# A fixed order, slot by slot, for the instructions of a block (convolution, two matrix products, SiLU)

## The chip, the cores and the metric

One core of one Trainium2 chip. The metric is the device time of one execution in microseconds (us). Engines: PE (TensorE) multiplies matrices into PSUM, which has eight banks of 128 x 512 float32; DVE (VectorE) and ACT (ScalarE) work elementwise and can read PSUM; POOL (GpSimd) and the DMA queues move and prepare data.

## The reference

The input `x` has 8 sequences of 4096 tokens with 192 channels. A causal convolution over 7 tokens has one set of softmax weights for each of 8 heads (24 channels each). Then, token by token:

```python
attn = lightweight_conv(x, softmax(weight))   # (32768, 192)
h = attn @ w_in                               # 192 -> 2048
g = h * (1 / (1 + exp(-h)))                   # SiLU
out = g @ w_out                               # 2048 -> 192
```

The weights `w_in` and `w_out` arrive as float64 and are rounded to float32 on the chip. All arithmetic is float32.

## The kernel before

The 32768 tokens are cut into 32 blocks of 1024. A block is two halves of 512 tokens, which stand side by side in the Strassen-like form in which both matrix products are computed: instead of 12 plain products for one row of chunks there are 11, of sums of inputs and sums of weights, and the results are sums of products again.

*Convolution* (`turn_in`, `conv`, `spread`). The input of the next block is loaded as 32 x 32 squares (`load`, 12 DMAs), turned by three DVE transposes, and its halo copied by a DMA (`xt<-xt`). `conv` runs 7 taps for each of three channel groups `k`, on DVE, each tap adding to the one before. `spread` copies a finished group by four DMAs into the tile `dup`. `win` makes four DVE differences of `dup` in the tile `win`. Before the change `conv` and `turn_in` are generators, stepped by the callers.

*First product* (`up`, line 343). For each of 8 chunks `m` there are 11 products named P1 to P7 and E11 to E22, each with 64 rows of the array; two of them, one in the upper and one in the lower half of the array, run at the same time as a pair. `ORDER` (line 75) lists 44 pairs. The products of one `m` go into three banks, "1", "b" and "d". Bank "1" grows from P1 by P6, P7, P4 and E21, and is copied to a buffer `u` after P1 (ACT), P6 (DVE) and P7 (ACT) (`snap`, lines 377 and 379); the next product of that bank has to wait for the copy. `total` (line 384) adds such a copy and bank "b" or "d" on DVE (line 386) and applies SiLU on ACT (line 387); the chunk in bank "1" itself goes through SiLU directly (line 396). The buffers `u` are 8.

*Second product* (`sum_g`, `down`, `merge`). For each of four pairs of chunks `j`, `sum_g` makes four DVE sums of g (1024 elements wide, line 427), and `down` multiplies 22 times into five banks `accs`, two matmuls at the same time in the left and right half of the array. `merge` combines the five banks by 7 ACT copies and 6 DVE sums into `cmb`; `store` turns it by three DVE transposes and stores it by 12 DMAs.

*What sets the order.* A scheduler places each instruction on its engine's queue by its priority and by when its inputs are expected; program order is only a preference. `fill` (line 530) hands out steps of `store`, `turn_in`, `conv` and `sum_g` after every second slot of ORDER; the rest of `conv`, `spread`, the next `load` and `win` stand between the four `down`s. Banks and buffers are given out in the order in which they are first written. Block 0 is special: its first product is plain (`up_plain`), mixed with the rounding of the weights (`rounded`), and its POOL sums of weights come later.

Of the kernel before, what the change touches and what calls it, by code (L numbers as in the profile page):

```python
# [17 lines left out]
def kernel(  # L18
# [238 lines left out]
    def turn_in(b):  # L257
        nat = nats[b]
        xt = xts[b] = xpool.tile([P, NK, pad + TB], F32, tag="xt", name="xt")
        if b * TT % S == 0:  # L260
            nc.gpsimd.memset(xt[0:R, :, 0:pad], 0.0)
        else:
            nc.gpsimd.tensor_copy(xt[0:R, :, 0:pad], tails.pop(b))
        for k in range(NK):
            nc.vector.transpose(
                xt[:, k, pad : pad + TB], nat[:, k, :, :].rearrange("p k c -> p (k c)")
            )
            yield
        nc.sync.dma_start(out=xt[R:P, :, 0:pad], in_=xt[0:R, :, TB : TB + pad])
        if (b + 1) * TT % S:  # L270
            tails[b + 1] = xpool.tile([R, NK, pad], F32, tag="tail", name="tail", bufs=2)
            nc.sync.dma_start(out=tails[b + 1], in_=xt[R:P, :, TB : TB + pad])

    def conv(b, k):

        src = xts[b][:, k, :]
        dst = nats[b][:, k, :, :].rearrange("p k c -> p (k c)")
        for i in range(K):
            tap = taps[:, k, i : i + 1]
            if i == 0:  # L280
                nc.vector.tensor_scalar(dst, src[:, 0:TB], scalar1=tap, scalar2=None, op0=ALU.mult)  # L281
            else:
                nc.vector.scalar_tensor_tensor(  # L283
                    out=dst, in0=src[:, i : i + TB], scalar=tap, in1=dst, op0=ALU.mult, op1=ALU.add
                )
            yield
# [14 lines left out]
    def win(b):  # L301

        d = dups[b]
        t = wins[b] = xpool.tile([P, 4, TB], F32, tag="win", name="win")
        for i, u, v in (
            (0, d[:, 1, 0, :], d[:, 0, 0, :]),
            (1, d[:, 1, 1, :], t[:, 0, :]),
            (2, d[:, 1, 1, :], d[:, 1, 0, :]),
            (3, d[:, 0, 1, :], t[:, 1, :]),
        ):  # L310
            nc.vector.tensor_tensor(t[:, i, :], u, v, op=ALU.subtract)
# [31 lines left out]
    def up(b, fill):  # L343


        d, t = dups[b], wins[b]
        bk, us, seen = {}, {}, set()

        def product(m, name):
            e, r, s = m % 2, wr[m // 2], ws[m // 2]  # L350

            other, bn, w, v = {
                "P1": (0, "1", r[:, 0, 0, :], d[:, 0, 0, :]),
                "P6": (0, "1", r[:, 0, 1, :], t[:, 1, :]),
                "P7": (0, "1", r[:, 1, 0, :], t[:, 2, :]),
                "P4": (0, "1", r[:, 1, 1, :], t[:, 3, :]),
                "E21": (0, "1", r[:, 1, 2, :], d[:, 0, 2, :]),
                "P2": (1, "b", s[:, 0, 1, :], d[:, 0, 1, :]),
                "E11": (1, "b", s[:, 0, 2, :], d[:, 0, 2, :]),
                "P5": (1, "d", s[:, 1, 0, :], t[:, 0, :]),  # L360
                "E22": (1, "d", s[:, 1, 2, :], d[:, 1, 2, :]),
                "P3": (1, "d", s[:, 0, 0, :], d[:, 1, 1, :]),
                "E12": (1, "d", s[:, 1, 1, :], d[:, 1, 2, :]),
            }[name]
            half = e ^ other
            first = (m, bn) not in bk
            if first:
                bk[m, bn] = bank()
# [5 lines left out]
        def snap(m, i):
            us[m, i] = upool.tile([P, TB], F32, tag="u", name="u")
            if i == 2:
                nc.vector.tensor_copy(us[m, i], bk[m, "1"])  # L377
            else:
                nc.scalar.copy(us[m, i], bk[m, "1"])  # L379

        def g_of(m, a, n):
            return g_tile(b, m // 2, a)[:, n, m % 2, :]

        def total(m, a, n, i, bn):
            g = g_of(m, a, n)
            nc.vector.tensor_tensor(g, us[m, i], bk[m, bn], op=ALU.add)  # L386
            nc.scalar.activation(g, g, AF.Silu)  # L387

        after = (
            (("P1",), lambda m: snap(m, 1)),  # L390
            (("P6",), lambda m: snap(m, 2)),
            (("P7",), lambda m: snap(m, 3)),
            (("E22", "P7"), lambda m: total(m, 1, 1, 3, "d")),
            (("P3", "E12"), lambda m: total(m, 0, 1, 2, "d")),
            (("E11", "P1"), lambda m: total(m, 0, 0, 1, "b")),
            (("E21", "P4"), lambda m: nc.scalar.activation(g_of(m, 1, 0), bk[m, "1"], AF.Silu)),  # L396
        )
        for i, slot in enumerate(ORDER.split(", ")):
            new = []
            for one in slot.split():  # L400
                name, m = one.split(".")
                product(int(m), name)
                new.append((int(m), name))
            seen.update(new)
            for needs, what in after:
                for m, name in new:
                    if name in needs and all((m, n) in seen for n in needs):
                        what(m)
            fill(i)

    sums = {}

    def sum_g(b, j):

        t = [tpool.tile([P, 2, 2 * TB], F32, tag="t", name="t") for _ in range(2)]
        sums[b, j] = t
# [4 lines left out]
        for out, u, v in (
            (t[0][:, 0, :], of(0, 1), of(0, 0)),
            (t[0][:, 1, :], of(1, 1), t[0][:, 0, :]),
            (t[1][:, 1, :], of(1, 0), t[0][:, 1, :]),
            (t[1][:, 0, :], of(1, 1), of(0, 1)),
        ):
            nc.vector.tensor_tensor(out, u, v, op=ALU.subtract)  # L427
            yield

    def down(b, j, accs):  # L430
        g = [gs.pop((b, j, a)) for a in range(2)]
        t = [s.rearrange("p i (e t) -> p i e t", e=2) for s in sums.pop((b, j))]
# [7 lines left out]

        for e in range(2):
            for a in range(2):
                for n in range(2):
                    mm(0, n, w[:, a, e, 2 * R : D], g[a][:, n, e, :], e == 0 and a == 0)
        for i, one, two in (
            (1, (w[:, 0, :, 0:R], g[0][:, 0]), (x_[:, 1], t[0][:, 1])),
            (2, (w[:, 1, :, 0:R], g[1][:, 0]), (w[:, 1, :, R : 2 * R], t[1][:, 1])),
            (3, (x_[:, 2], g[1][:, 1]), (x_[:, 0], t[0][:, 0])),
        ):
            for e in range(2):  # L450
                for half, (lhs, rhs) in enumerate((one, two)):
                    mm(i, half, lhs[:, e, :], rhs[:, e, :], e == 0)
        for e in range(2):
            mm(4, e, w[:, 0, e, R : 2 * R], t[1][:, 0, e, :], True)
# [133 lines left out]
```

## Time and profile before

| | |
|---|---|
| median of 3 runs | 3277.9 us (3275.98 to 3287.45) |
| profiled execution | 3288.16 us, span 3286.4 us |
| PE busy | 2882.4 us, 88% |
| DVE busy | 2049.5 us, 62% |
| ACT busy | 1013.4 us, 31% |
| POOL busy | 57.4 us, 2% |
| mean granted clock of TensorE | 0.929 of full speed |

The profile shows one execution. Its span goes from the first to the last instruction. Matmuls are pipelined and their ends are modelled, so a busy PE need not be at full speed. PEld is the load of weights into the array, which overlaps the matmuls. An idle time is put down to the instruction whose end released it. L369 are the matmuls of `up`, L436 those of `down`, L331 those of block 0's `up_plain`.

### The profile page before, as it was taken

What the parts mean: (1) busy time and instruction counts of PE and PEld (TensorE: products, weight loads), DVE (VectorE), ACT (ScalarE), POOL (GpSimd) and SP (SyncE); (2) the same over time, 40 slices, a digit from 0 to 9 for tenths busy, and PEclk for the clock granted to TensorE, in tenths of its full rate; (3) what the DMA queues carried; (4) which work ended last, traced back from release to release, by engine and by line L of the source; (5) the groups of instructions that cost most, each with busy time, mean ns of one, the idle gap of its engine ahead of it and who ended that gap; (6) DMA issues with size and microseconds to landing.
All of it is one profiled execution on the core that took longest, in us unless ns stands there. A gap on an engine that the chain in (4) does not pass through costs nothing.

```text
span 3286.4 us, 29826 instructions
## 1 busy us (share of the span) xinstructions
PE 2882.4 (88%) x11280; PEld 1169.8 (36%) x11280; DVE 2049.5 (62%) x2758; ACT 1013.4 (31%) x1763; POOL 57.4 (2%) x105
## 2 busy tenths in 40 slices
PE   3998889888898988989888999889998898988998
PEld 2333333333333333333333333333333333333333
DVE  8756666656657566666566665665656657566644
ACT  2233322323322333223232223332233322333222
POOL 5100000000000000000000000000000000000000
PEclk9999998998999999999999999998999999999989
DMA  6211112211022110221111221102212022110110
GB/s 135 39 33 36 23 26 39 39 29 33 16 39 39 33 36 10 39 39 33 36 28 21 39 39 30 37 11 39 39 29 38 11 39 39 33 36 17 32 29 10
DMA packets 451296, 110.79 MB, mean 34 GB/s; under 512 B 423952, under 2 KB 424848, under 8 KB 451152
## 3 DMA queue, kind: packets, MB, share of 16 engines
q1 hardware_dynamic: 447872, 101.00, 16.7%
q0 software_dynamic: 1664, 5.51, 0.6%
q10 hardware_dynamic: 1616, 2.39, 0.3%
q8 instruction: 88, 1.44, 0.2%
q14 instruction: 56, 0.46, 0.0%
HBM read 31.49 MB, written 25.17 MB: 17 GB/s over the span
## 4 chain that ended last, share of the span: by engine, by line
PE 60%; DVE 31%; issue 5%; ACT 3%; DMA 1%; SPq 0%; DVEq 0%; ACTq 0%
PE ps L436 31%; PE ps L369 29%; DVE nat L283 11%; DVE t L427 5%; DVE g L386 4%; DVE u L377 4%; DVE cmb L463 2%; DVE u L463 2%; ACT g L387 1%; DVE nat L281 1%; DVE osb L485 1%; PE ps L331 1%; ACT u L379 1%; DMA nat<-in_x_dram 1%; ACT cmb L465 0%
## 5 line engine op out<-in xcount | busy, mean ns | idle before, releaser
L369 PE MATMUL ps<-dup,ws 64*128 64x512 f32 x2480 | 980.6, 625 | 0.0
L369 PE MATMUL ps<-win,wr 64*128 64x512 f32 x1488 | 761.4, 723 | 230.8 <-DVE u L377 206.8
L436 PE MATMUL ps<-g,wo 128*64 128x512 f32 x3072 | 901.4, 593 | 0.0
L386 DVE TENSOR_TENSOR g<-u,ps 128x512 f32<-128x512 f32 x744 | 495.5, 683 | 640.9 <-PE ps L369 547.9
L387 ACT ACTIVATE g<-g 128x512 f32<-128x512 f32 x744 | 465.9, 630 | 513.5 <-DVE g L386 504.8
L369 PE MATMUL ps<-dup,wr 64*128 64x512 f32 x992 | 566.8, 710 | 22.0 <-ACT u L379 20.5
L369 PEld LDWEIGHTS ps<-dup,ws 64*128 64x128 f32 x2480 | 406.3, 202 | 307.7 <-issue 285.4
L427 DVE TENSOR_TENSOR t<-g,t 128x1024 f32<-128x1024 f32 x256 | 313.4, 1224 | 292.0 <-PE ps L436 288.7
L436 PEld LDWEIGHTS ps<-g,wo 128*64 128x64 f32 x3072 | 284.5, 137 | 590.7 <-issue 567.2
L436 PE MATMUL ps<-t,wx 128*64 128x512 f32 x1024 | 481.2, 592 | 0.0
L369 PEld LDWEIGHTS ps<-win,wr 64*128 64x128 f32 x1488 | 284.1, 225 | 539.2 <-DVE u L377 281.0
L379 ACT COPY u<-ps 128x512 f32<-128x512 f32 x496 | 278.6, 583 | 508.2 <-DVE g L386 451.8
L283 DVE SCALAR_TENSOR_TENSOR nat<-xt,taps,nat 128x512 f32<-128x512 f32 x576 | 415.9, 745 | 6.4
L436 PE MATMUL ps<-t,wo 128*64 128x512 f32 x1024 | 372.1, 592 | 0.0
L369 PE MATMUL ps<-win,ws 64*128 64x512 f32 x496 | 292.3, 690 | 89.5 <-DVE g L386 89.5
L427 DVE TENSOR_TENSOR t<-g 128x1024 f32<-128x1024 f32 x256 | 304.9, 1222 | 43.1 <-ACT g L387 43.1
L465 ACT COPY cmb<-ps 128x512 f32<-128x512 f32 x32 | 18.7, 585 | 971.9 <-PE ps L436 971.9
L369 PEld LDWEIGHTS ps<-dup,wr 64*128 64x128 f32 x992 | 188.0, 217 | 203.9 <-issue 93.2
L436 PE MATMUL ps<-g,wx 128*64 128x512 f32 x512 | 240.6, 592 | 0.0
L396 ACT ACTIVATE g<-ps 128x512 f32<-128x512 f32 x248 | 142.4, 593 | 106.4 <-PE ps L369 102.9
L377 DVE COPY u<-ps 128x512 f32<-128x512 f32 x248 | 166.4, 681 | 0.0
L369 PEld LDWEIGHTS ps<-win,ws 64*128 64x128 f32 x496 | 88.9, 200 | 169.7 <-DVE g L386 115.1
(60 smaller groups left out, 1043.5 us busy)
## 6 DMA issues: line engine op xcount, KB each, us to landing
dup<-nat SPq DMA_DIRECT2D x384, 128.0 KB, 2.3
nat<-in_x_dram SPq DMA_DIRECT2D x384, 64.0 KB, 2.5
out_dram<-osb SPq DMA_DIRECT2D x384, 64.0 KB, 1.9
raw<-in_moe_w_out_dram POOLq DMA_DIRECT2D x8, 384.0 KB, 4.2
raw<-in_moe_w_in_dram POOLq DMA_DIRECT2D x12, 192.0 KB, 4.2
ws<-wr ACTq DMA_DIRECT2D x8, 192.0 KB, 4.3
raw<-in_moe_w_in_dram ACTq DMA_DIRECT2D x4, 192.0 KB, 8.0
xt<-xt SPq DMA_DIRECT2D x32, 4.5 KB, 1.9
```

The source lines that it names most:

```text
L281: nc.vector.tensor_scalar(dst, src[:, 0:TB], scalar1=tap, scalar2=None, op0=ALU.mult)
L283: nc.vector.scalar_tensor_tensor(out=dst, in0=src[:, i : i + TB], scalar=tap, in1=dst, op0=ALU.mult, op1=ALU.add)
L331: nc.tensor.matmul(hs[a, n, e], rows(wr[j], e)[:, a, k, :], rows(d, e)[:, n, k, :], start=k == 0, stop=k == NK - 1,)
L369: nc.tensor.matmul(bk[m, bn], rows(w, half), rows(v, half), start=first, stop=True, skip_group_check=True,)
L377: nc.vector.tensor_copy(us[m, i], bk[m, "1"])
L379: nc.scalar.copy(us[m, i], bk[m, "1"])
L386: nc.vector.tensor_tensor(g, us[m, i], bk[m, bn], op=ALU.add)
L387: nc.scalar.activation(g, g, AF.Silu)
L396: (("E21", "P4"), lambda m: nc.scalar.activation(g_of(m, 1, 0), bk[m, "1"], AF.Silu)),
L427: nc.vector.tensor_tensor(out, u, v, op=ALU.subtract)
L436: nc.tensor.matmul(accs[i][R * half : R * half + R, :], lhs, rhs, start=first and j == 0, stop=j == NJ - 1, skip_group_check=True,)
L463: nc.vector.tensor_tensor(out, u, v, op=ALU.add)
```

## The change

The order of a block is written out in one text, PLAN, of 88 slots: 44 for `up`, 44 for `down`. A slot names two products of `up`, or stands for two matmuls of `down`, and then the DVE and ACT instructions that follow them: `s` copies a bank, `C` adds, `g` applies SiLU, `t` is a sum of g, `i` and `v` are transposes and taps of the next block, `w` its window, `M`, `z`, `y`, `c` the merge, `o` an output transpose with its stores. A minus sign means the block before. `pin` ties each of these instructions behind the one traced before it on its engine, so that the queue has the order of the text. The products are in a new order, the buffers `u` are 13, the banks of `down` are taken when first used, and the last steps of a merge stand in the first slots of the next block's `up`. In block 0 the roundings are placed one ahead of each `up_plain`.

```diff
-    upool = ctx.enter_context(tc.tile_pool(name="up", bufs=8))
+    upool = ctx.enter_context(tc.tile_pool(name="up", bufs=13))
...
+    PLAN = (
+        "P1.0 P1.1 -z7.0 -M3.0 | P1.2 P5.0 s1.1 -M4.0 | P5.1 E22.0 s1.0 -M5.0 s1.2 | "
+        "E22.1 P6.1 -M6.0 | P6.0 P1.3 s2.1 | P6.2 P5.2 -o.0 s1.3 s2.0 | P5.3 P7.1 s2.2 | "
+        "P7.0 E22.2 -o.1 s3.1 | P7.2 P6.3 i.0 s3.0 C22.1 | E22.3 E21.1 s3.2 s2.3 | "
+        "P4.0 P4.1 g22.1 C22.0 | E12.1 P7.3 C22.2 g22.0 | E21.0 E12.0 i.1 C21.1 s3.3 i.2 | "
+        "E21.2 E12.2 C21.0 C22.3 | P3.1 P3.0 g22.2 | P4.2 P4.3 g22.3 C12.0 | "
+        "E12.3 P2.0 C12.1 g12.0 | P2.1 E11.0 v.00 C21.2 v.01 g12.1 | E11.1 E21.3 C11.0 | "
+        "P1.4 P1.5 v.02 C21.3 | P1.6 P3.2 g11.0 C11.1 s1.4 | P3.3 P5.4 C12.2 s1.5 | "
...
+        "E11.7 P3.6 C12.7 g11.6 | C11.7 g12.7 | C12.6 g11.7 v.11 | g12.6 t.02 | . | v.12 | "
+        "v.13 v.14 | v.15 | v.16 | v.20 | t.10 | t.11 | . | t.13 | v.21 | v.22 | v.23 | "
+        "t.12 | v.24 | v.25 | v.26 | t.20 | t.21 | . | t.23 | t.22 | t.30 | . | t.31 | w.0 | "
+        "w.1 | w.2 | w.3 | t.33 | t.32 | . | . | . | cE.0 | o.2 | y1.0 | z1.0 z6.0 | "
+        "z4.0 M2.0 | M1.0 | z5.0"
     )
+
+    def pin(ins):
+        return tc.keep_in_program_order(ins)
...
+    def begin_down(b):
+        did.add((b, "down"))
+        for k in range(NK):
+            if b + 1 < NB and (b, f"v.{k}{K - 1}") in did:
+                spread(b + 1, k)
...
+    for k in range(NK):
+        turn_in(0, k)
+    round_in(0)
+    for k in range(NK):
+        for i in range(K):
+            conv(0, k, i)
+        spread(0, k)
+        if k == 0:
+            load_in(2, nc.gpsimd)
+    load(1)
+    round_in(1)
+    load_in(3, nc.gpsimd)
+    for j in range(NJ):
+        up_plain(0, j)
+        if j + 2 < NJ:
+            round_in(j + 2)
+            load_out(j, nc.gpsimd)
+        else:
+            round_out(j + 2 - NJ)
+            combine_out(j + 2 - NJ)
+            if j == 2:
+                load_out(2, nc.gpsimd)
+    load_out(3, nc.gpsimd)
+    for j in range(2, NJ):
+        round_out(j)
+        combine_out(j)
+    run(0, [[t for t in s if t[0] in "tiv"] for s in plan[:NU]])
+    for j in range(NJ):
+        combine_in(j)
+
     for b in range(NB):
...
+        if b:
+            run(b, plan[:NU])
+        begin_down(b)
+        slots = (None for j in range(NJ) for _ in down(b, j))
+        for s in plan[NU:]:
+            next(slots)
+            run(b, [s])
+        assert next(slots, 0) == 0
+    run(NB, plan[:NU])
```

After the third group's last tap (`v.26`) the next block's `load` is issued. The slots left out go on in the same way.

## Rows read from the trace of the kernel before

**Rows 1.** The page: busy times by engine, and the chain that ended last.
```profile
PE 2882.4 (88%) x11280; PEld 1169.8 (36%) x11280; DVE 2049.5 (62%) x2758; ACT 1013.4 (31%) x1763; POOL 57.4 (2%) x105
...
PE 60%; DVE 31%; issue 5%; ACT 3%; DMA 1%; SPq 0%; DVEq 0%; ACTq 0%
```
**Rows 2.** The chain in order of time (start, us, what): `down` of blocks 0, 1, 31.
```profile
101.06 37.92 PE ps L436 x176
...
203.22 31.93 PE ps L436 x148
...
3237.41 33.65 PE ps L436 x156
```
**Rows 3.** Windows (length, busy us of each engine, PEclk, DMA): `up`, then `down`, one block.
```profile
1251.80:1314.90 63.10, 51.78 (x178) 23.35 (x176) 40.98 (x60) 26.90 (x48) 0.19 (x1) 0.89 0.05 9
1314.90:1352.80 37.90, 37.90 (x177) 12.55 (x176) 22.09 (x27) 4.68 (x9) 0.00 (x0) 1.00 0.37 70
```
**Rows 4.** The timeline (start, us, engine, line): first matmuls of two neighbouring groups of `down`.
```profile
1324.42 4.03 PE L436 MATMUL ps<-g,wo 128*64 128x512 f32 x17
...
1333.86 4.03 PE L436 MATMUL ps<-g,wo 128*64 128x512 f32 x17
```
**Rows 5.** The waits of that block (us in total, times, longest): PE's.
```profile
PE ps L369 <- DVE u L377: 6.9, 3, 3.9
...
PE ps L369 <- DVE g L386: 3.0, 1, 3.0
...
PE ps L369 <- ACT u L379: 1.4, 2, 0.8
```
**Rows 6.** Windows of 4 us inside that `up`.
```profile
1268.50:1272.50 4.00, 2.56 (x5) 1.40 (x6) 3.23 (x6) 2.31 (x5) 0.19 (x1) 0.55 0.00 0
1280.50:1284.50 4.00, 3.35 (x13) 1.37 (x10) 1.59 (x3) 1.29 (x3) 0.00 (x0) 1.00 0.00 0
1304.50:1308.50 4.00, 4.00 (x10) 1.59 (x12) 1.99 (x4) 2.44 (x4) 0.00 (x0) 0.50 0.00 0
```
**Rows 7.** The timeline of that `up`: taps, a sum, and PE behind them.
```profile
1263.95 5.34 DVE L283 SCALAR_TENSOR_TENSOR nat<-xt,taps,nat 128x512 f32<-128x512 f32 x7
...
1269.21 0.68 DVE L386 TENSOR_TENSOR g<-u,ps 128x512 f32<-128x512 f32 x1
...
1269.94 1.22 PE L369 MATMUL ps<-win,ws 64*128 64x512 f32 x1 [3.01 <-DVE g L386]
```
**Rows 8.** Groups by line and form, whole span (busy us, mean ns | idle before): DVE's kinds.
```profile
L386 DVE TENSOR_TENSOR g<-u,ps 128x512 f32<-128x512 f32 x744 | 495.5, 683 | 640.9 <-PE ps L369 547.9 <-ACT u L379 91.1
...
L283 DVE SCALAR_TENSOR_TENSOR nat<-xt,taps,nat 128x512 f32<-128x512 f32 x576 | 415.9, 745 | 6.4
...
L427 DVE TENSOR_TENSOR t<-g,t 128x1024 f32<-128x1024 f32 x256 | 313.4, 1224 | 292.0 <-PE ps L436 288.7
...
L377 DVE COPY u<-ps 128x512 f32<-128x512 f32 x248 | 166.4, 681 | 0.0
...
L485 DVE STREAM_TRANSPOSE osb<-cmb 128x512 f32<-128x512 f32 x96 | 64.5, 697 | 62.1 <-ACT cmb L465 61.2
...
L281 DVE TENSOR_SCALAR nat<-xt,taps 128x512 f32<-128x512 f32 x96 | 42.7, 472 | 3.2 <-DMA xt<-xt 3.2
```
**Rows 9.** The page: DMA issues (KB each, median us to landing).
```profile
dup<-nat SPq DMA_DIRECT2D x384, 128.0 KB, 2.3
nat<-in_x_dram SPq DMA_DIRECT2D x384, 64.0 KB, 2.5
...
xt<-xt SPq DMA_DIRECT2D x32, 4.5 KB, 1.9
```
**Rows 10.** Windows of block 0: until PE starts, then until `down` begins.
```profile
0.00:42.80 42.80, 0.00 (x0) 0.03 (x1) 28.44 (x50) 6.26 (x8) 14.68 (x30) 1.00 0.58 117
42.80:101.00 58.20, 50.25 (x194) 25.91 (x194) 56.66 (x72) 25.02 (x42) 35.43 (x41) 0.94 0.44 105
```
**Rows 11.** The timeline: PE's last matmuls.
```profile
3274.30 1.03 PE L436 MATMUL ps<-t,wo 128*64 128x512 f32 x4
```

More of the change, by code (lines that the diff above doesn't have):

```diff
@@ L1 @@
 from contextlib import ExitStack
-from itertools import chain
 import concourse.bass as bass
@@ L255 @@
     tails = {}
[L257 to L261, printed above, removed]
-        else:
[L263 to L266, printed above, removed]
-            )
[L268 to L286, printed above, removed]
+    def turn_in(b, k):
+        if k == 0:
+            xt = xts[b] = xpool.tile([P, NK, pad + TB], F32, tag="xt", name="xt")
+            if b * TT % S == 0:
+                nc.gpsimd.memset(xt[0:R, :, 0:pad], 0.0)
+            else:
+                nc.gpsimd.tensor_copy(xt[0:R, :, 0:pad], tails.pop(b))
+        xt = xts[b]
+        pin(
+            nc.vector.transpose(
+                xt[:, k, pad : pad + TB], nats[b][:, k, :, :].rearrange("p k c -> p (k c)")
+            )
+        )
+        if k == NK - 1:
+            nc.sync.dma_start(out=xt[R:P, :, 0:pad], in_=xt[0:R, :, TB : TB + pad])
+            if (b + 1) * TT % S:
+                tails[b + 1] = xpool.tile([R, NK, pad], F32, tag="tail", name="tail", bufs=2)
+                nc.sync.dma_start(out=tails[b + 1], in_=xt[R:P, :, TB : TB + pad])
@@ L288, in spread, with conv @@
+    def conv(b, k, i):
+        src = xts[b][:, k, i : i + TB]
+        dst = nats[b][:, k, :, :].rearrange("p k c -> p (k c)")
+        tap = taps[:, k, i : i + 1]
+        if i == 0:
+            pin(nc.vector.tensor_scalar(dst, src, scalar1=tap, scalar2=None, op0=ALU.mult))
+        else:
+            pin(
+                nc.vector.scalar_tensor_tensor(
+                    out=dst, in0=src, scalar=tap, in1=dst, op0=ALU.mult, op1=ALU.add
+                )
+            )
     def spread(b, k):
@@ L299, with win @@
     dups, wins = {}, {}
-    def win(b):
+    def win(b, i):
         d = dups[b]
[L304 to L311, printed above, removed]
+        if i == 0:
+            wins[b] = xpool.tile([P, 4, TB], F32, tag="win", name="win")
+        t = wins[b]
+        u, v = (
+            (d[:, 1, 0, :], d[:, 0, 0, :]),
+            (d[:, 1, 1, :], t[:, 0, :]),
+            (d[:, 1, 1, :], d[:, 1, 0, :]),
+            (d[:, 0, 1, :], t[:, 1, :]),
+        )[i]
+        pin(nc.vector.tensor_tensor(t[:, i, :], u, v, op=ALU.subtract))
     def rows(t, e):
@@ L341, in up_plain, with product @@
                     nc.scalar.activation(g[:, n, e, :], hs[a, n, e], AF.Silu)
-    def up(b, fill):
+    bk, us, sums, cmbs, accs = {}, {}, {}, {}, {}
+    def product(b, m, name):
         d, t = dups[b], wins[b]
[L347 to L368, printed above, removed]
@@ new lines, in product @@
+        e, r, s = m % 2, wr[m // 2], ws[m // 2]
+        other, bn, w, v = {
+            "P1": (0, "1", r[:, 0, 0, :], d[:, 0, 0, :]),
+            "P6": (0, "1", r[:, 0, 1, :], t[:, 1, :]),
+            "P7": (0, "1", r[:, 1, 0, :], t[:, 2, :]),
+            "P4": (0, "1", r[:, 1, 1, :], t[:, 3, :]),
+            "E21": (0, "1", r[:, 1, 2, :], d[:, 0, 2, :]),
+            "P2": (1, "b", s[:, 0, 1, :], d[:, 0, 1, :]),
+            "E11": (1, "b", s[:, 0, 2, :], d[:, 0, 2, :]),
+            "P5": (1, "d", s[:, 1, 0, :], t[:, 0, :]),
+            "E22": (1, "d", s[:, 1, 2, :], d[:, 1, 2, :]),
+            "P3": (1, "d", s[:, 0, 0, :], d[:, 1, 1, :]),
+            "E12": (1, "d", s[:, 1, 1, :], d[:, 1, 2, :]),
+        }[name]
@@ L369, in product @@
+        half = e ^ other
+        first = (b, m, bn) not in bk
+        if first:
+            bk[b, m, bn] = bank()
+        pin(
             nc.tensor.matmul(
-                bk[m, bn], rows(w, half), rows(v, half), start=first, stop=True,
+                bk[b, m, bn], rows(w, half), rows(v, half), start=first, stop=True,
                 skip_group_check=True,
             )
[L374 to L396, printed above, removed]
-        )
@@ L398, in up @@
[L398 to L416, printed above, removed]
+        )
@@ new lines, in g_of, with sums_h @@
+    def g_of(b, m, a, n):
+        return g_tile(b, m // 2, a)[:, n, m % 2, :]
+    def sums_h(b, name, m):
+        if name[0] == "s":
+            u = us[b, m, name[1]] = upool.tile([P, TB], F32, tag="u", name="u")
+            copy = nc.vector.tensor_copy if name == "s2" else nc.scalar.copy
+            pin(copy(u, bk[b, m, "1"]))
+            return
+        g = g_of(b, m, int(name[1]) - 1, int(name[2]) - 1)
+        if name == "C21":
+            pin(nc.scalar.activation(g, bk[b, m, "1"], AF.Silu))
+        elif name[0] == "g":
+            pin(nc.scalar.activation(g, g, AF.Silu))
+        else:
+            i, bn = {"C11": ("1", "b"), "C22": ("3", "d"), "C12": ("2", "d")}[name]
+            pin(nc.vector.tensor_tensor(g, us.pop((b, m, i)), bk[b, m, bn], op=ALU.add))
@@ L418, in of, with sum_g @@
+    def sum_g(b, j, i):
+        t = sums.setdefault((b, j), {})
+        if i // 2 not in t:
+            t[i // 2] = tpool.tile([P, 2, 2 * TB], F32, tag="t", name="t")
         def of(a, n):
             return gs[b, j, a][:, n, :, :].rearrange("p e t -> p (e t)")
[L421 to L428, printed above, removed]
@@ L430, in down @@
-    def down(b, j, accs):
-        g = [gs.pop((b, j, a)) for a in range(2)]
-        t = [s.rearrange("p i (e t) -> p i e t", e=2) for s in sums.pop((b, j))]
+        u, v = (
+            (lambda: (of(0, 1), of(0, 0))),
+            (lambda: (of(1, 1), t[0][:, 0, :])),
+            (lambda: (of(1, 1), of(0, 1))),
+            (lambda: (of(1, 0), t[0][:, 1, :])),
+        )[i]()
+        pin(nc.vector.tensor_tensor(t[i // 2][:, i % 2, :], u, v, op=ALU.subtract))
+    def down(b, j):
+        if j == 0:
+            accs[b] = []
+        g = [gs[b, j, a] for a in range(2)]
@@ L433, in down, with t @@
         w, x_ = wo[j], wx[j]
+        def t(i):
+            return sums[b, j][i // 2][:, i % 2, :].rearrange("p (e t) -> p e t", e=2)
         def mm(i, half, lhs, rhs, first):
-            nc.tensor.matmul(
-                accs[i][R * half : R * half + R, :], lhs, rhs,
-                start=first and j == 0, stop=j == NJ - 1, skip_group_check=True,
-            )
[L441 to L449, printed above, removed]
-            for e in range(2):
[L451 to L454, printed above, removed]
@@ L557 @@
-    run(store(NB - 1))
+            pin(
+                nc.tensor.matmul(
+                    accs[b][i][R * half : R * half + R, :], lhs, rhs,
+                    start=first and j == 0, stop=j == NJ - 1, skip_group_check=True,
+                )
+            )
+        for i in range(5):
+            if j == 0:
+                accs[b].append(bank())
+            for e in range(2):
+                if i == 0:
+                    for a in range(2):
+                        for n in range(2):
+                            mm(0, n, w[:, a, e, 2 * R : D], g[a][:, n, e, :], e == 0 and a == 0)
+                        yield
+                elif i < 4:
+                    one, two = {
+                        1: ((w[:, 0, :, 0:R], g[0][:, 0]), (x_[:, 1], t(1))),
+                        2: ((w[:, 1, :, 0:R], g[1][:, 0]), (w[:, 1, :, R : 2 * R], t(3))),
+                        3: ((x_[:, 2], g[1][:, 1]), (x_[:, 0], t(0))),
+                    }[i]
+                    for half, (lhs, rhs) in enumerate((one, two)):
+                        mm(i, half, lhs[:, e, :], rhs[:, e, :], e == 0)
+                    yield
+                else:
+                    mm(4, e, w[:, 0, e, R : 2 * R], t(2)[:, e, :], True)
@@ new lines, in down, with merge @@
+        for a in range(2):
+            del gs[b, j, a]
+        yield
+    def merge(b, name):
+        lo, hi = slice(0, R), slice(R, P)
+        acc = accs[b]
+        if b not in cmbs:
+            cmbs[b] = [xpool.tile([P, NK, TB], F32, tag="cmb", name="cmb"), None, None]
+        cmb = cmbs[b][0]
+        for i, first in ((1, ("z6", "z1")), (2, ("z5", "z7"))):
+            if name in first and cmbs[b][i] is None:
+                cmbs[b][i] = upool.tile([P, TB], F32, tag="u", name="u")
+        z, zz = cmbs[b][1:]
+        copies = {
+            "cE": lambda: (cmb[:, 2, :], acc[0]),
+            "z6": lambda: (z[lo], acc[1][hi]),
+            "z1": lambda: (z[hi], acc[1][lo]),
+            "y1": lambda: (cmb[lo, 0, :], acc[1][lo]),
+            "z4": lambda: (cmb[hi, 0, :], acc[2][hi]),
+            "z5": lambda: (zz[lo], acc[3][hi]),
+            "z7": lambda: (zz[hi], acc[4][lo]),
+        }
+        adds = {
+            "M1": lambda: (z, z, acc[1]),
+            "M2": lambda: (cmb[lo, 0, :], cmb[lo, 0, :], acc[2][lo]),
+            "M3": lambda: (z, z, zz),
+            "M4": lambda: (z[hi], z[hi], acc[4][hi]),
+            "M5": lambda: (cmb[:, 1, :], z, acc[3]),
+            "M6": lambda: (cmb[hi, 0, :], cmb[hi, 0, :], z[hi]),
+        }
+        if name in copies:
+            pin(nc.scalar.copy(*copies[name]()))
+        else:
+            out_, u, v = adds[name]()
+            pin(nc.vector.tensor_tensor(out_, u, v, op=ALU.add))
@@ new lines, with turn_out @@
+    osbs = {}
+    def turn_out(b, i):
+        if b not in osbs:
+            osbs[b] = xpool.tile([P, NK, TB // SQ, SQ], F32, tag="osb", name="osb")
+        osb = osbs[b]
+        pin(
+            nc.vector.transpose(
+                osb[:, i, :, :].rearrange("p k c -> p (k c)"), cmbs[b][0][:, i, :]
+            )
+        )
+        for q in range(P // SQ):
+            n, c = (i, SQ * q) if i < 2 else (q // 2, P + SQ * (q % 2))
+            nc.sync.dma_start(
+                out=out_v[2 * b + n][:, :, c : c + SQ], in_=osb[SQ * q : SQ * q + SQ, i, :, :]
+            )
@@ new lines, with step @@
+    plan = [slot.split() for slot in PLAN.split("|")]
+    NU = len(plan) // 2
+    did = set()
+    def step(b, token):
+        if token[0] == "-":
+            b, token = b - 1, token[1:]
+        name, arg = token.split(".") if "." in token else ("", "")
+        if b < 0 or b >= NB or not name or (b, token) in did:
+            return
+        did.add((b, token))
+        digits = [int(c) for c in arg]
+        if name[0] in "PE":
+            product(b, digits[0], name)
+        elif name[0] in "sCg":
+            if b:
+                sums_h(b, name, digits[0])
+        elif name == "t":
+            sum_g(b, *digits)
+        elif name[0] in "Mzyc":
+            merge(b, name)
+        elif name == "o":
+            turn_out(b, *digits)
+        elif b + 1 < NB:
+            {"i": turn_in, "v": conv, "w": win}[name](b + 1, *digits)
+            if name == "v" and digits[1] == K - 1 and (b, "down") in did:
+                spread(b + 1, digits[0])
+                if digits[0] == NK - 1 and b + 2 < NB:
+                    load(b + 2)
@@ new lines, in begin_down, with run @@
+    def begin_down(b):
[3 more added lines that the diff above has]
+                spread(b + 1, k)
+    def run(b, slots):
+        for s in slots:
+            for token in s:
+                step(b, token)
+    for k in range(NK):
[5 more added lines that the diff above has]
+        spread(0, k)
+        if k == 0:
+            load_in(2, nc.gpsimd)
```

93 lines of the change are left out of this document (2 added, 91 removed), and 18 rows, old and new, of tables (ORDER, PLAN).

## The prediction

> **What bounds the kernel now.** I read the page's busy shares first, then the chain that ended last, then one block cut into its two halves, then the waits inside it. The shares name PE as the fullest engine, with DVE behind it, and the chain puts 60% of the span on PE and 31% on DVE [rows 1]: PE sets the end, and DVE interrupts it. The chain in order of time gives the shape. Between the `down` of block 1 and that of block 31 lie (3237.41 - 203.22) / 30 = 101.1 us per block [rows 2]. The two halves of a block are not alike. `down` takes 37.9 us and PE is busy for all of it at a granted clock of 1.00; `up` has the same number of matmuls and takes 63.1 us at a mean clock of 0.89 [rows 3]. The two neighbouring groups of matmuls in `down` start 9.44 us apart [rows 4]: 11 pairs of products, so 0.858 us for a pair. `up` has 44 pairs too and would need 37.8 us. So each block loses 63.1 - 37.8 = 25.3 us, all in `up`.
>
> Three things make up the loss. PE waits 6.9 us for copies out of PSUM on DVE, 3.0 us for sums on DVE and 1.4 us for copies on ACT [rows 5]: 11.3 us. After the longer waits the granted clock falls to 0.50 to 0.55 of full speed, that is to 1.2 GHz, and comes back later [rows 6]; 11% of 63.1 us is another 6.9 us. The remaining 7 us are pairs that run out of step after a wait. The cause stands in DVE's order of work: seven convolution taps in a row keep it for 5.34 us while a sum (L386) that PE needs stands behind them; PE starts 0.05 us after that sum, having waited 3.01 us [rows 7]. These taps belong to the next block, whose `up` begins at 1352.8 [rows 3], over 80 us later. DVE is not too slow, it does 63.1 us of work in a block of 101 [rows 3]; it does it in the wrong order. The list ORDER spreads the taps over `up`, but the run shows them bunched: the issue order is not the order written.
>
> **The change, part by part.** *The pins and the list.* No instruction of a block is added or taken away. Per block DVE has 8 copies at 0.681, 24 sums at 0.683, 16 sums of g at 1.22, 18 taps at 0.745, 3 first taps at 0.472, and 16 others (6 merges, 6 transposes, 4 windows) at about 0.69 us [rows 8]: 5.4 + 16.4 + 19.6 + 13.4 + 1.4 + 11.0 = 67.3 us against 88 slots of PE, 88 x 0.858 = 75.5 us. So PE remains the bound if DVE never keeps it waiting. I added the list's DVE work slot by slot: 35.8 us in the 44 slots of `up` (37.8 us) and 31.5 us in the 44 of `down`, where slots 78 to 80 have none. DVE's sum stays behind PE's clock at every slot, and by the end of the block 8 us are free, so that a delay isn't handed on to the next block.
>
> *The tightest place*, worked by hand, time from the first slot of `up`. The last accumulator is done with the slot before, z7 on ACT takes to 0.8, then DVE runs M3, M4, M5, M6 to 3.6. s2.1 follows P6.1 (slot 3, done at about 3.6) and ends at 4.3, o.0 at 5.0, s2.0 at 5.7. P7.0 stands in slot 7, at 6.0 us, and waits for s2.0: 0.3 us to spare. M5 frees the bank that slot 6 takes at 2.9 us, against 5.1. The same hand-over in the trace costs 0.05 us [rows 7]. The other waits of the list have more room (P1.5 in slot 19 takes the bank that C12.1, three slots earlier in the list, frees).
>
> *What stalls remain.* Below: none, since DVE's records are counted at their full length and neighbours overlap (63.1 us measured for the 67.3). Above: if each of DVE's 85 instructions gave up another 0.05 us, DVE would need 71.6 us; over slots 0 to 63, where it has 52.7 of 54.9 us, it would fall 1 to 2 us behind, and the skew of a pair or two doubles that, so 4 us a block. I take 0.7 us, near the lower end, because the nearest row of a hand-over is 0.05 us and the list leaves slack at all places but one: 76.2 us a block.
>
> *Buffers for sums, 8 to 13.* They let P1, P6 and P7 copies live until their late C sums. No cost of their own; they are what allows E products 10 slots after P products.
>
> *Merge moved under the next `up`, banks taken one by one.* z7 and M3 to M6 now run in slots 0 to 3 of the next block instead of beside conv taps; counted above.
>
> *DMAs.* Their number per block stays: 12 spreads, 12 loads, 12 stores, and the halo. What each lands for is farther off than its time. The last spread follows v.26 in slot 63 and is wanted in slot 2 of the next block, 23 us later, against 2.3 us to land; the load follows it and is wanted at i.0, 28 us later, against 2.5 us [rows 9]. The halo xt<-xt is the one new narrow wait: issued after i.2 (slot 12), wanted by v.00 in slot 17, 4.3 us later, against 1.9 us [rows 9]. If it is late, C11.0, v.02 and C11.1 are queued behind v.00 on DVE, and the banks of slots 20 and 21 behind those. On SP the halo stands behind the stores of o.0 and o.1 (slots 5 and 7), which are issued by then. I cost it at nothing.
>
> *The first block.* Here the order changes as well: all 21 taps come before the second weight rounding, one `round_in` ahead of each `up_plain`. PE now starts at 42.8 us [rows 10]; taps in one run of 15 us behind the first rounding would let it start near 31. But DVE bounds this stretch: it is busy 28.4 + 56.7 = 85 us before `down` begins at 101 [rows 10, 2], and some 6 us of that (two sums of g, four or five taps) move behind. From 13 us on without a gap that is 92 us. Bounds: 20 us gained if PE's earlier start decides, 10 us lost if the pinned taps hold up a rounding that PE waits for. I take 9 us gained, so that block 1 begins at 130 instead of 139.
>
> *The end.* From PE's last matmul to the end were 11 us [rows 11]; five merge steps, two transposes and the stores remain, 9 us.
>
> **The sum** against the profiled execution (130 for the first block, 31 blocks, the end): 130 + 31 x 76.2 + 9 = 2501 us of span, plus the 1.8 us by which its 3288.2 us exceeds its span: 2503. The median before is 0.3% under the profiled execution, which would make it 2495. I say 2500.
>
> [...] A matmul stretch with PE busy 3.35 of 4 us kept the clock at 1.00, while stretches in or after idle times of 3 us were granted 0.55 and 0.50 [rows 6]. [...]
>
> **Rivals.**
> 1. *DVE still holds PE up.* The list is exact to fractions of a microsecond and the chip is not; a late bank makes one product of a pair wait and the pairs run out of step as now. At 4 to 8 us a block: 79.5 to 83.5, 2605 to 2729 us. For it: 95% of DVE's time in `up` is booked. Against: DVE's 8 us of slack at each block's end, and a hand-over of 0.05 us.
> 2. *The clock still falls.* If the 6.9 us of lost clock stay although the long waits go: 31 x (76.2 + 6.9) + 141 = 2717 us. Against: the 0.85 busy stretch at full clock.
> 3. *Slower.* A strictly ordered DVE stands at v.00 until the halo has landed, and everything behind it waits. In the trace 11.3 us of waiting cost 25.3 us with clock and skew, so that is 2.24 us for each; from 75.5 to 101.1 us a block it takes 25.6 / 2.24 = 11.4 us of this one wait, a landing of 4.3 + 11.4 = 15.7 us. At 13 us of wait: 75.5 + 29 = 104.6 a block, about 3385. Against: a median of 1.9 us.
> 4. *The pins change nothing*, because the bunched order comes from something other than the scheduler's freedom: within 0.5% of 3278. Against: the taps ran ahead of their written place, so that freedom is what let them.
>
> **How the numbers follow.** Forecast 0.74, rival 1 0.16, rival 2 0.05, rival 3 0.03, rival 4 0.02. The forecast's own range: 31 x 75.5 + 119 + 8 + 2 = 2470 below, and 2 us of stalls a block with a first block that gains nothing, 31 x 77.5 + 139 + 11 + 2 = 2555, above. To leave out no more than 2 in 10, the range takes in the 4 us bound of the stalls with a first block at its worse bound, 31 x 79.5 + 149 + 11 + 2 = 2627: 2465 to 2630. Faster by over 0.5% (what a measurement of this kernel can tell from no change) 0.95, within 0.5% 0.02, slower 0.03.
>
> **What would show it.** Right: `up` and `down` both near 38 us, clock 1.00 in both, PE's wait for DVE copies and sums under 1 us a block, single taps between sums instead of seven in a row, DVE over 80% busy. Wrong: a repeated gap before P7.0 (tightest place), DVE idle before v.00 on the halo (rival 3), a clock of 0.5 with no wait of 2 us near it (rival 2), `up` over 42 us (rival 1), or block 1 later than 139 us.

## The result and the profile after

The changed kernel takes 2504.1 us (median of 4 runs, 2503.7 to 2505.1) against 3279.0 us (median of 4 runs of the kernel before): a ratio of 0.763, 95% interval 0.762 to 0.765. The profiled execution has a span of 2502.0 us and a mean clock of 0.997. In the new kernel L385 are the matmuls of `up`, L440 those of `down`, L349 those of `up_plain`, L400 the copies, L409 the sums, L299 the taps, L426 the sums of g, L502 and L499 the merge, L511 the output transposes.

The page of the new kernel, its busy times and its chain, against [rows 1]:

```profile
PE 2439.5 (98%) x11280; PEld 953.7 (38%) x11280; DVE 2056.0 (82%) x2758; ACT 980.1 (39%) x1763; POOL 71.4 (3%) x105
...
PE 97%; DVE 2%; DMA 1%; issue 0%; ACTq 0%; SPq 0%; POOL 0%; ACT 0%; DVEq 0%
```

DVE does the same work (2056 us for 2050), but its share of the chain fell from 31% to 2%, all of it in block 0 and behind the last matmul. The chain in order of time (start, us, what) alternates two pieces and nothing else from 101 us to the last matmul, against [rows 2]:

```profile
66.22 34.38 PE ps L349 x153
100.60 37.92 PE ps L440 x176
138.52 37.97 PE ps L385 x176
176.49 37.92 PE ps L440 x176
...
2453.03 37.94 PE ps L440 x176
```

A block takes (2453.03 - 100.60) / 31 = 75.88 us, where it took 101.1. The two halves in windows, against [rows 3], and the only row of waits that the matmuls have in the whole run (four waits, all in block 0, before 66.3 us):

```profile
1200.90:1238.90 38.00, 38.00 (x180) 16.98 (x180) 33.14 (x50) 25.48 (x47) 0.00 (x0) 1.00 0.09 15
1238.90:1276.80 37.90, 37.90 (x178) 12.54 (x178) 30.12 (x35) 4.97 (x9) 1.07 (x1) 1.00 0.37 70
```

```profile
PE ps L349 <- DMA dup<-nat: 51.3, 4, 43.9
```

`up` fell from 63.1 to 38.0 us at a clock of 1.00; `down` did not change. What replaced the seven taps in a row of [rows 7] is seen in DVE's timeline, where the taps of `up` (L296, L299) stand one or two at a time between sums:

```profile
1214.06 1.28 DVE L409 TENSOR_TENSOR g<-u,ps 128x512 f32<-128x512 f32 x2 [1.21 <-PE ps L385]
1215.26 0.48 DVE L296 TENSOR_SCALAR nat<-xt,taps 128x512 f32<-128x512 f32 x1
1215.78 0.75 DVE L299 SCALAR_TENSOR_TENSOR nat<-xt,taps,nat 128x512 f32<-128x512 f32 x1
1216.61 0.69 DVE L409 TENSOR_TENSOR g<-u,ps 128x512 f32<-128x512 f32 x1
1217.21 0.74 DVE L299 SCALAR_TENSOR_TENSOR nat<-xt,taps,nat 128x512 f32<-128x512 f32 x1
1217.88 0.68 DVE L409 TENSOR_TENSOR g<-u,ps 128x512 f32<-128x512 f32 x1
```

### The profile page after: what moved, and what is told of

It is laid out like the page before. It is cut to its first block, busy times and chain, and to the rows that moved or that the text cites. A ratio compares the mean times of both kernels' runs of the same rounds, so it can differ in the third digit from the quotient of the medians.

```text
span 2502.0 us, 29772 instructions
## 1 busy us (share of the span) xinstructions
PE 2439.5 (98%) x11280; PEld 953.7 (38%) x11280; DVE 2056.0 (82%) x2758; ACT 980.1 (39%) x1763; POOL 71.4 (3%) x105
## 4 chain that ended last, share of the span: by engine, by line
PE 97%; DVE 2%; DMA 1%; issue 0%; ACTq 0%; SPq 0%; POOL 0%; ACT 0%; DVEq 0%
PE ps L440 48%; PE ps L385 47%; PE ps L349 1%; DVE nat L299 1%; DMA raw<-in_moe_w_in_dram 0%; DVE two L183 0%; DMA dup<-nat 0%; DMA xt<-xt 0%; DVE mh L180 0%; DVE two L176 0%; ACTq L146 0%; DVE mh L171 0%; DVE two L164 0%; DVE two L165 0%; SPq L311 0%
## 5 line engine op out<-in xcount | busy, mean ns | idle before, releaser
L440 PE MATMUL ps<-g,wo 128*64 128x512 f32 x3072 | 901.4, 593 | 0.0
L385 PE MATMUL ps<-dup,ws 64*128 64x512 f32 x2480 | 869.9, 589 | 0.0
L409 DVE TENSOR_TENSOR g<-u,ps 128x512 f32<-128x512 f32 x744 | 488.5, 680 | 117.0 <-PE ps L385 103.2
L385 PE MATMUL ps<-win,wr 64*128 64x512 f32 x1488 | 567.7, 589 | 0.0
L440 PEld LDWEIGHTS ps<-g,wo 128*64 128x64 f32 x3072 | 284.5, 137 | 590.7 <-issue 567.2
L440 PE MATMUL ps<-t,wx 128*64 128x512 f32 x1024 | 481.2, 592 | 0.0
L406 ACT ACTIVATE g<-g 128x512 f32<-128x512 f32 x744 | 445.6, 631 | 88.1 <-DVE g L409 88.1
L385 PEld LDWEIGHTS ps<-dup,ws 64*128 64x128 f32 x2480 | 363.0, 187 | 292.0 <-issue 284.7
L499 ACT COPY cmb<-ps 64x512 f32<-64x512 f32 (+1 forms) x96 | 55.8, 581 | 997.5 <-PE ps L440 996.7
L299 DVE SCALAR_TENSOR_TENSOR nat<-xt,taps,nat 128x512 f32<-128x512 f32 x576 | 431.8, 750 | 11.1
L385 PE MATMUL ps<-dup,wr 64*128 64x512 f32 x992 | 419.9, 596 | 0.0
L440 PE MATMUL ps<-t,wo 128*64 128x512 f32 x1024 | 372.2, 592 | 0.0
L426 DVE TENSOR_TENSOR t<-g,t 128x1024 f32<-128x1024 f32 x256 | 313.4, 1224 | 68.0 <-PE ps L440 57.0
L400 ACT COPY u<-ps 128x512 f32<-128x512 f32 x496 | 277.8, 589 | 233.3 <-PE ps L385 233.3
L426 DVE TENSOR_TENSOR t<-g 128x1024 f32<-128x1024 f32 x256 | 308.9, 1218 | 0.0
L385 PEld LDWEIGHTS ps<-win,wr 64*128 64x128 f32 x1488 | 233.4, 187 | 175.3 <-issue 146.7
L385 PE MATMUL ps<-win,ws 64*128 64x512 f32 x496 | 242.2, 589 | 0.0
L440 PE MATMUL ps<-g,wx 128*64 128x512 f32 x512 | 240.6, 592 | 0.0
L385 PEld LDWEIGHTS ps<-dup,wr 64*128 64x128 f32 x992 | 160.5, 187 | 127.4 <-issue 120.1
L400 DVE COPY u<-ps 128x512 f32<-128x512 f32 x248 | 166.3, 680 | 9.8 <-PE ps L385 5.9
L440 PEld LDWEIGHTS ps<-t,wx 128*64 128x64 f32 x1024 | 140.3, 137 | 0.0
```

What stands on the lines that cost most here:

```text
L299: nc.vector.scalar_tensor_tensor(out=dst, in0=src, scalar=tap, in1=dst, op0=ALU.mult, op1=ALU.add)
L385: nc.tensor.matmul(bk[b, m, bn], rows(w, half), rows(v, half), start=first, stop=True, skip_group_check=True,)
L400: pin(copy(u, bk[b, m, "1"]))
L406: pin(nc.scalar.activation(g, g, AF.Silu))
L409: pin(nc.vector.tensor_tensor(g, us.pop((b, m, i)), bk[b, m, bn], op=ALU.add))
L426: pin(nc.vector.tensor_tensor(t[i // 2][:, i % 2, :], u, v, op=ALU.subtract))
```

## The experiments

The change has three parts that can be taken apart: pins, the new list, and the buffers. The first two groups below do that; the third tests the prediction's prices; the last tries to gain more.

### Which part carries the gain

**No pins.** The new list and 13 buffers, all pins out:

```diff
     def pin(ins):
-        return tc.keep_in_program_order(ins)
+        return ins
```

> All pins removed; the list, the 13 buffers and the program order stay. Theory (DVE's issue order is what cost the time): the scheduler bunches the next block's taps again, PE waits for DVE in `up`, 15 to 30 us a block come back: 2970 to 3430 us. Rival (the new order of products and the buffers are what helps, the scheduler follows them by itself): 2504 to 2560 us.

Measured: 2893.4 us (ratio to before 0.882, 0.881 to 0.883). Between the two forecasts: 389 us of the 775 come back, less than the theory said. A block is 88.4 us. PE issues its matmuls in exactly the order of the pinned kernel; the queues of DVE and ACT differ. The window of one `up` with a window of 4 us inside it, and PE's two waits:

```profile
933.80:984.60 50.80, 45.81 (x178) 22.26 (x180) 40.68 (x60) 26.21 (x47) 0.11 (x1) 0.90 0.06 11
...
942.00:946.00 4.00, 3.52 (x6) 1.34 (x8) 4.00 (x7) 0.58 (x1) 0.00 (x0) 0.50 0.59 101
```

```profile
942.48 3.14 PE L385 MATMUL ps<-win,wr 64*128 64x512 f32 x3 [2.50 <-DVE u L400]
...
965.55 1.22 PE L385 MATMUL ps<-win,wr 64*128 64x512 f32 x1 [2.49 <-DVE u L400]
```

`up` is long again, PE waits for DVE copies, and the clock drops to 0.50 behind the first wait of 2.50 us.

**Only DVE free, and only DVE pinned.**

```diff
     def pin(ins):
+        if ins.ins.engine == mybir.EngineType.DVE:   # the other run: !=
+            return ins
         return tc.keep_in_program_order(ins)
```

> DVE's instructions are left to the scheduler, those of PE and ACT stay pinned. Theory: nearly as slow as with no pin at all, within 3% of it, since DVE's order alone makes PE wait. Rival (PE's and ACT's order carry the gain): within 3% of 2504 us.

> The reverse: only DVE's instructions are pinned, PE and ACT are left to the scheduler. Theory: within 1% of 2504 us. Rival: over 2700 us.

Measured: 2843.6 us with DVE free, 2526.1 us with DVE alone pinned. The theory holds in both: DVE free is 1.7% from no pins at all, DVE alone is 0.9% from the full change. DVE's queue carries the effect; pins on ACT and PE are worth 22 us (`up` 38.66 us instead of 37.97). PE's queue has the same order in all these kernels, so the 22 us are ACT's.

**The old list, pinned.** The kernel before with its own list, each PE, DVE and ACT instruction of a block wrapped in `pin`, and 13 buffers (in strict order more than eight copies are alive at once, so eight were not tried):

```diff
-    upool = ctx.enter_context(tc.tile_pool(name="up", bufs=8))
+    upool = ctx.enter_context(tc.tile_pool(name="up", bufs=13))
...
-            nc.vector.tensor_tensor(g, us[m, i], bk[m, bn], op=ALU.add)
-            nc.scalar.activation(g, g, AF.Silu)
+            pin(nc.vector.tensor_tensor(g, us[m, i], bk[m, bn], op=ALU.add))
+            pin(nc.scalar.activation(g, g, AF.Silu))
```

> The kernel before with its old list and program order, but pinned on PE, DVE and ACT as written, and 13 buffers. By its list DVE has 40 us of work in `up` (6 merge sums, 8 copies, 24 sums, 6 transposes, 7 taps, 4 sums of g) against 37.9 us of PE, so pins alone can't reach 37.9: I expect 43 to 50 us for `up`, 2700 to 2920 us. Rival A (pins alone do it): 2504 to 2560. Rival B (pins do nothing without the new list): 3200 to 3350.

Measured: 2524.0 us (0.769, 0.768 to 0.771). My expectation was wrong, 176 us too long at its lower end, and rival A right: pins and buffers alone bring all but 20 us; these 20 us are the worth of everything else together (the list, the moved merge, block 0). My count of 40 us of DVE work in `up` missed that the work isn't tied to the half in which it is written: the window shows 31.4 us of it, as two merge sums already run in `down` and three sums and one sum of g run over into the next one, without PE waiting:

```profile
369.30:407.70 38.40, 38.34 (x179) 16.95 (x179) 31.36 (x49) 24.30 (x45) 0.00 (x0) 1.00 0.13 22
```

**The buffers alone,** and **the new list alone** (8 buffers, no pins):

```diff
-    upool = ctx.enter_context(tc.tile_pool(name="up", bufs=8))
+    upool = ctx.enter_context(tc.tile_pool(name="up", bufs=13))
```

> The kernel before with 13 buffers for sums instead of 8, nothing else. Theory: within 1.5% of 3279 us, DVE's order stays as it is. Rival (ACT's copies waited for buffers, 452 us in all in the trace of before, and that held PE): under 3000 us.

> The new list and program order with no pins and 8 buffers for sums: the fourth corner beside before (old list, 8 buffers, 3279), old list with 13 (3080) and new list with 13 (2893), all unpinned. If list and buffers help each by itself, about 190 us each: 3080 to 3100 us. If the new list needs the buffers: over 3200.

Measured: 3079.7 us for the buffers alone (0.939, 0.936 to 0.941), and 3124.7 us for the list alone, a little above the first of its two forecasts. I expected nothing from the buffers and was wrong, though the rival's 3000 us was not reached either: ACT's copies waited for DVE's sums, the instructions that free a buffer. The waits of the kernel before (us in total, times, longest) have this row, and with 13 buffers there is none of it:

```profile
ACT u L379 <- DVE g L386: 451.8, 124, 9.4
```

The waits that the profile gives the matmuls of `up` fell by less than the time did, from 342 to 285 us in all; how the rest of the 199 us reached PE was not traced.

The whole table (us):

| | 8 buffers | 10 | 13 |
|---|---|---|---|
| old list, free | 3279 | | 3080 |
| new list, free | 3125 | | 2893 |
| old list, pinned | | | 2524 |
| new list, pinned | | 2504 | 2504 |

With 10 buffers:

> The changed kernel with 10 buffers for sums instead of 13. By the pinned list a buffer is free again whenever the next copy wants it, so nothing waits: 2504 us within 0.2%. Rival (the further buffers are what lets the list run): over 2530 us.

Measured: 2504.2 us, as expected; all queues have the same order as with 13. So with free queues list and buffers give about 150 to 230 us each; with pinned queues the list's share shrinks to 20 us, and three of the 13 buffers are not used for time. What pins would do with eight buffers is not shown.

### What a wait costs

**Seven taps in one slot, and twelve.** The pins stay; only their places in the list change (the second run also moves v.10 to v.14 into slot 17):

```diff
-        ... | P2.1 E11.0 v.00 C21.2 v.01 g12.1 | ...
+        ... | P2.1 E11.0 v.00 v.01 v.02 v.03 v.04 v.05 v.06 C21.2 g12.1 | ...
```

> The changed kernel with the seven taps of group 0 in one slot (17) instead of spread over slots 17 to 32; pins stay. By the list DVE then reaches s2 and the sums behind the taps about 4 us late, and P6.4 in slot 22 waits some 2.5 us for a bank copy. If a wait costs only itself: 31 x 2.5 = 77 us, 2580 us. If it costs 2.24 times that, as in the trace of before, with clock and skew: 31 x 5.6, 2677 us. If bunching is harmless: 2504.

> As the kernel with seven bunched taps, but twelve in slot 17 (the seven of group 0 and five of group 1). By the list the copy s1.4 comes so late that P6.4 waits about 5.9 us a block. If a wait costs only itself, as 2.5 us did: 31 x 5.9 = 184 us, 2688 us at a clock of 1.00. If a wait of this length also brings the clock down, as in the trace of before (6.9 us of lost clock for two such waits, 3.4 each): 31 x 9.4 = 290 us, 2795 us, with stretches granted 0.5.

Measured: 2583.2 us with seven (78.44 us a block, 2.56 more) and 2754.4 us with twelve (83.94 a block, 8.06 more). Bunched taps alone, in an otherwise good order, bring back PE's waits. With seven, the two windows around a wait stay at clock 1.00; below them stand the matmuls of slots 21 and 22 that came late, with the wait:

```profile
550.00:554.00 4.00, 3.31 (x14) 1.15 (x10) 3.86 (x6) 0.60 (x1) 0.00 (x0) 1.00 0.00 0
554.00:558.00 4.00, 3.55 (x14) 1.55 (x16) 3.23 (x6) 3.58 (x7) 0.00 (x0) 1.00 0.00 0
```

```profile
554.44 1.12 PE L385 MATMUL ps<-win,ws 64*128 64x512 f32 x2 [1.13 <-DVE g L409]
555.57 0.69 PE L385 MATMUL ps<-win,wr 64*128 64x512 f32 x1
```

The profile's wait is 1.13 us, less than half of the 2.56 us that a block lost. Only one product of slot 21 (P5.4) had to wait for DVE; the other had run before it, so the two halves of the array worked one after the other, and P6.4 in slot 22 began 2.42 us later than in the changed kernel. The 2.5 us of the expectation are this lateness; the profile counts only the time in which neither half worked.

The clock did not stay up in every block. In 28 of the 30 blocks with this wait every window read is at 1.00; in two the same wait is followed by half speed, and these blocks are 1.5 and 1.7 us longer than the others:

```profile
1338.57 1.30 PE L385 MATMUL ps<-win,ws 64*128 64x512 f32 x2 [1.13 <-DVE g L409]
```

```profile
1340.00:1344.00 4.00, 4.00 (x14) 1.69 (x14) 1.69 (x3) 2.19 (x5) 0.00 (x0) 0.65 0.00 0
```

With twelve, PE waits 5.80 us and is then at half speed for some 6 us, 0.50 and 0.64 as the means of two windows (timeline, then windows):

```profile
585.01 1.22 PE L385 MATMUL ps<-win,wr 64*128 64x512 f32 x1 [5.80 <-ACT u L400]
```

```profile
584.00:588.00 4.00, 2.99 (x8) 1.45 (x10) 2.30 (x4) 3.49 (x7) 0.00 (x0) 0.50 0.00 0
588.00:592.00 4.00, 4.00 (x14) 1.60 (x14) 0.69 (x1) 0.95 (x2) 0.00 (x0) 0.64 0.00 0
592.00:596.00 4.00, 4.00 (x22) 1.76 (x20) 3.65 (x6) 1.93 (x5) 0.00 (x0) 1.00 0.02 4
```

The rest of `up` behind this wait took 20.6 to 22.0 us, where it takes 19.1 at full clock: 1.5 to 3.0 us for the drop. So the second theory's 3.4 us was too much, but its sign right. My factor of 2.24 was loss by the profile's wait. Taken so it is 2.56 / 1.13 = 2.27 with seven, where one half of the array stood still, and 8.06 / 5.80 = 1.39 with twelve, where both halves waited together. It held for the first and not for the second. A wait that "costs only itself" is right for seven only if the lateness of P6.4 is meant.

**The tightest place,** o.1 moved ahead of s2.0:

```diff
-P6.2 P5.2 -o.0 s1.3 s2.0 | P5.3 P7.1 s2.2 | P7.0 E22.2 -o.1 s3.1 |
+P6.2 P5.2 -o.0 s1.3 -o.1 s2.0 | P5.3 P7.1 s2.2 | P7.0 E22.2 s3.1 |
```

> The changed kernel with one output transpose (o.1) moved ahead of s2.0, the place that I worked out as the tightest (0.3 us to spare). The copy ends at 6.4 us of the block, P7.0 stands at 6.0: a wait of about 0.45 us a block, 31 x 0.45 = 14 us, 2518 us. If there is more room than I worked out: 2504.

Measured: 2517.4 us, 76.31 us a block, 0.43 more (the profile shows a wait of at most 0.2 us). The hand count of that place was right to a tenth of a microsecond. It can be read off the changed kernel: `up` begins at 1200.9, and DVE's M6, s2.1, o.0, s2.0 (with s2.2) come one after the other, s2.0 ending about 5.7 us in:

```profile
1203.80 0.69 DVE L502 TENSOR_TENSOR cmb<-cmb,u 64x512 f32<-64x512 f32 x1
...
1204.62 0.69 DVE L400 COPY u<-ps 128x512 f32<-128x512 f32 x1
...
1205.34 0.71 DVE L511 STREAM_TRANSPOSE osb<-cmb 128x512 f32<-128x512 f32 x1
...
1205.97 1.25 DVE L400 COPY u<-ps 128x512 f32<-128x512 f32 x2
```

**The halo wanted at once,** v.00 right behind i.2:

```diff
-E21.0 E12.0 i.1 C21.1 s3.3 i.2 | ... | P2.1 E11.0 v.00 C21.2 v.01 g12.1 |
+E21.0 E12.0 i.1 C21.1 s3.3 i.2 v.00 | ... | P2.1 E11.0 C21.2 v.01 g12.1 |
```

> The changed kernel with the first tap v.00 right behind the last input transpose i.2 (slot 12) instead of in slot 17: DVE stands at it until the halo DMA has landed, 1.9 to 2.4 us, and everything behind it is late. By the list PE then waits about 1.8 us at E12.3: 31 x 1.8 = 56 us, 2560 us; with clock and skew as in the trace of before 2630 us. If DVE's slack absorbs it: 2504.

Measured: 2523.2 us, 76.50 a block, 0.62 more where I expected 1.8. DVE does stand still for the landing, 2.06 us; PE shows a wait of 0.36 us behind it:

```profile
458.11 0.49 DVE L296 TENSOR_SCALAR nat<-xt,taps 128x512 f32<-128x512 f32 x1 [2.06 <-DMA xt<-xt]
...
459.24 2.41 PE L385 MATMUL ps<-dup,ws 64*128 64x512 f32 x9 [0.36 <-DVE g L409]
```

Some 1.4 us of DVE's wait was covered. I had taken 2.4 us for the landing and records at full length. The mechanism of rival 3 exists, at a price far from what it needs to decide.

### More gain in block 0

```diff
     def rounded(dst, key):
...
-        nc.vector.tensor_single_scalar(ex, hi, 0x7FF * one, op=ALU.bitwise_and)
+        pin(nc.vector.tensor_single_scalar(ex, hi, 0x7FF * one, op=ALU.bitwise_and))
```

and so for each DVE instruction of the rounding.

> The changed kernel with the DVE instructions of the weight rounding pinned as well, so that the roundings of the second and later weights can't slip between the taps of block 0. In the trace of the changed kernel the 21 taps take from 32.4 to 60.1 us that way and PE works without a gap only from 66.2 us. Theory: the taps end some 10 us earlier, PE runs through from about 50 us, block 1 begins some 13 us earlier: 2491 us. Rival (DVE's total before the first `down` decides, whatever its order): 2500 to 2508. Other rival (a rounding is now late for `up_plain`): over 2510.

Measured: 2502.6 us (5 runs, ratio to before 0.763, 0.762 to 0.764), not to be told from the change by the ratios' intervals. Its runs (2502.2 to 2503.3) lie some 1.6 us below those of the kernel with 10 buffers, which ran beside it (2504.0 to 2504.5). PE does start at 30.8 us instead of 43.9, but it then waits for ACT and, at the first `down`, for DVE's sums of g; block 1 begins at 137.1 instead of 138.5:

```profile
30.82 10.09 PE L349 MATMUL ps<-dup,wr 64*128 64x512 f32 x32 [30.82 <-DMA dup<-nat]
...
101.89 0.61 PE L440 MATMUL ps<-t,wx 128*64 128x512 f32 x1 [1.11 <-DVE t L426]
```

The rival's time came out. That DVE's total decides and not its order fits, but is not shown apart: in this run DVE itself stood still for 3.0 us for a weight's DMA (until 54.4 us) and 2.0 us for the halo. No version was found that is clearly faster than the change.

## Why the prediction was right, point by point

*The cause in DVE's order*: right, and shown three ways: with the list and the buffers in place DVE's pins alone come within 1% of the change, DVE alone set free loses 340 of the 775 us, and seven taps put in one slot bring PE's waits back. *But what made the order good was mispriced.* I spoke of the list's slots as if they carried the gain; pinning the old list, with 13 buffers, does nearly as well. And I gave the buffers no effect of their own; with free queues they were worth 199 us.

*The floor of a pair*, 0.858 us: 37.97 and 37.92 us for 44 pairs are 0.863 and 0.862. I took it between two groups inside `down`, and inside both halves it holds (42 pairs of one `up` start within 36.05 us, 0.858 each); the two changes between `up` and `down` cost 0.15 to 0.2 us each, which I had at nothing. 31 x 88 x 0.0045 = 12 us too little.

*Remaining stalls*, 0.7 us a block: none at all, 22 us too much. The list left DVE enough slack that no lateness shows at PE. The two bounds were 0 and 4 us; the lower one was the answer.

*The first block*, 9 us gained: 0.5 us. PE started at 43.9, not near 31, because the pins tie the taps to each other and not the roundings, which are free and slipped between them. DVE's timeline of block 0 in the changed kernel (a rounding step L180, L183 on either side of each tap), and where PE at last runs through:

```profile
33.00 0.94 DVE L180 SCALAR_TENSOR_TENSOR mh<-mh,two 128x768 f32<-128x768 int32 x1
33.87 0.73 DVE L299 SCALAR_TENSOR_TENSOR nat<-xt,taps,nat 128x512 f32<-128x512 f32 x1
34.53 0.94 DVE L183 SCALAR_TENSOR_TENSOR two<-raw,two 128x768 int32<-128x768 int32 x1
...
66.22 34.38 PE L349 MATMUL ps<-dup,wr 64*128 64x512 f32 x154 [0.82 <-DMA dup<-nat]
```

The last group's copy to `dup` was issued only at 60.1 us, when the last tap was done. With that undone in the last experiment, DVE still held `down` back: the sum of g that PE waits for came at 101.9 us, four slots (3.4 us) into `down`, so even then 98 us and not the 92 that I gave to DVE.

*The end*, 9 us: 11, as before; I shortened it without a row to stand on.

The errors are -12, +22, -8.5 and -2 us: they cancel, and the forecast of 2501 us of span against 2502.0 is closer than its terms deserve.

*The rivals.* In the changed kernel neither clock nor waits stayed (rivals 1 and 2), DVE did not stand at v.00 (rival 3), and 4 did not happen.

*Waits and the clock.* I had read half speed as what comes after the longer waits. The runs don't bear that out. Half speed followed waits of 1.13 us (seven taps, two blocks of 30), 1.63 us (DVE free, at 521.3 us), 2.50 us (no pins) and 5.80 us (twelve taps). It did not follow the same 1.13 us in the other 28 blocks, 2.59 us with no pins at 171.2 us, or 2.78 us in the very `up` of the kernel before that I had read:

```profile
1259.98 0.69 PE L369 MATMUL ps<-win,wr 64*128 64x512 f32 x1 [2.78 <-DVE u L377]
```

```profile
1260.50:1264.50 4.00, 3.73 (x14) 1.35 (x12) 4.00 (x8) 0.63 (x1) 0.00 (x0) 1.00 0.48 83
```

The length of a wait alone doesn't tell what the clock does. The Trainium skill ("TensorE: Matmul & The Clock Gate", section "A second HAM failure mode: psum-queue depth-cycling") tells of a bf16 kernel that cycles through PSUM banks and in which PE idles so often for moments between groups of matmuls that the clock swings between its two levels. The trace with seven taps agrees in part, with half speed behind 1.13 us in two blocks; waits of 0.2 and 0.4 us in every block (the tightest place, the halo) left every window of the steady blocks at 1.00. Half speed behind a short wait is the mechanism of rival 2; in the changed kernel no such wait is left.

What stays open: why the scheduler put the taps forward (only the order that it made was seen, not its reasons), and what besides a wait's length decides whether the clock falls.

## What to carry to other kernels

When the fullest engine waits and its helper is idle over a third of the time, compare the helper's issue order in the timeline with the order written; here the free scheduler put next-block work ahead of what the bound engine needed at once. Pin the helper's queue first, with the buffers that a strict order needs (556 of the 775 us here came with the pins of the old list, 199 with its buffers), and only then tune the order itself. Pins hold only what they are put on: unpinned work goes between pinned instructions.
